# A fused attention and SiLU feed-forward kernel: the first two units of tokens take the ff chunks in two halves, and 14 instead of 10 heads stay in plain float32

## The chip, the cores and the metric

The kernel runs on one core of one Trainium2 chip. The metric is the device time of one execution in microseconds (us), lower is better. The kernel before took 1336.0 us as the median of three runs (1329.97 to 1337.23).

## The reference, cut to what matters

```python
# q, k, v: (8, 8, 576, 64); M_prev: (8, 8, 64, 64); z_prev: (8, 8, 64); beta: (8,)
scores = scale * np.matmul(q, k.transpose(0, 1, 3, 2))      # causal mask
a = np.exp(scores - max); a /= a.sum(-1, keepdims=True) + 1e-09
local = np.matmul(a, v)
q_p = phi(q)                                                # elu + 1
mem_out = einsum(q_p, M_prev) / (einsum(q_p, z_prev) + 1e-06)
attn = g * mem_out + (1 - g) * local                        # g = sigmoid(beta), per head
x = attn.transpose(0, 2, 1, 3).reshape(4608, 512)
h = x @ w_in                                                # 512 x 2048
out = (h * sigmoid(h)) @ w_out                              # 2048 x 512, float32
```

The weights `w_in` and `w_out` arrive as 64-bit floats; everything else is float32.

## The kernel before, in words

There are 64 heads (8 batches of 8), and one head is one round of `attention()`. In the same round the first part of head n (`scores`: transposes of q and k, score matmuls, mask and row minimum, exponentials, row sums, scaling) is interleaved with the second part of head n-1 (`values`: transposes of the probabilities, product with v and with M_prev, result into `xt`). One round is 10 steps of the generator.

A head is made in one of two ways. A **whole** head (the first `N_WHOLE`) keeps float32 operands: two matmul instructions stand for each float32 product, and there is little elementwise work. Its score matmuls have k and q transposed in 64 rows (`qf`, `tt[0:64]`). A **split** head writes each operand as a high and a low fp32r part, stacked to 128 rows (`kk`, `qq`, `ql`, `ph`, `pl`, `vs`, `qp`): fewer TensorE cycles, but more work on ScalarE (ACT), VectorE (DVE) and GpSimd (POOL).

The feed-forward part (`ffn()`) works on units of 256 tokens, 18 units in all. A unit goes over 8 pairs of ff chunks. One pair is 24 matmuls into `h` (L552, 128x256), then tanh on ACT (L563), one operation on DVE (L564), one on POOL (L567), one on DVE (L568), and 12 matmuls into `acc` (L532, 128x512). I call these 36 matmuls one **FFN step**; a unit is 8 steps. A unit needs all heads of the batches that its tokens lie in: units 0 and 1 need the first 8 heads, units 2 and 3 the first 16, units 4 and 5 the first 24, and so on (`heads_needed`).

Before any chunk of weights is used it is **prepared** (`split_weight`): its 64-bit words are turned into float32 and split into a high and a low part. There are 32 such chunks, 16 of `w_in` and 16 of `w_out`, each with three operations on DVE (L152, L154, L159), three on ACT (L150, L158, L161) and two on POOL (L156, L162). 12 of the 32 do not stay on the chip: they go to DRAM and come back for every use through two buffers named `flow`.

The order of the work is set in two places. The loop at the end of the function paces the three generators against each other: `PREP_RATE` chunks are prepared per 9 attention steps, `FFN_RATE` and `FIRST_RATE` say how many FFN steps go with an attention step. A scheduler then lays the recorded instructions out into one fixed order for each engine. All DMAs are issued from one queue (SP).

Of the kernel before, what the change touches and what calls it, by code (L numbers as in the profile page):

```python
# [8 lines left out]
F32 = mybir.dt.float32  # L9
# [3 lines left out]
AF = mybir.ActivationFunctionType  # L13
ALU = mybir.AluOpType
# [11 lines left out]
NB = dict(vs=1, e=2, r=1, qp=1, ms=2, raw=1, qn=2, mr=3, zb=2, st=2, nrm=2, ph=2, pl=2, xb=1, tt=2)  # L26
PS_S, PS_T, PS_X, PS_H = 2, 2, 1, 1
FIRST_STEPS = 1
N_WHOLE = 10
ROW_BUFS = 4  # L30
W_AHEAD = 2
PREP_RATE = 3.0
PREP_AFTER = 3.0
FFN_RATE = 0.22
FIRST_RATE = 0.2
FIRST_UNITS = 2
W_EARLY = 2

# [2 lines left out]
def memory_attention_then_silu_ffn(ctx, tc, q, k, v, M_prev, z_prev, beta, w_in, w_out, out):  # L41
    nc = tc.nc
    B, H, S, D = q.shape
    NT, DM = out.shape
    DFF = w_in.shape[1]
    P = 128
# [94 lines left out]
    def split_weight(kind, c, raw):  # L141
# [24 lines left out]
    ready, anchor = set(), {}  # L166


    order = [
        (kind, 2 * x + j) for p in range(NP + 1) for kind, x in (("i", p), ("o", p - 1))  # L170
        if 0 <= x < NP for j in range(2)]
    loaded = []

    def load_next(n):
# [40 lines left out]
    def scores(b, h, raw, rest, made, whole):  # L215
# [5 lines left out]
        anchor["dve"] = nc.vector.transpose(out=tt, in_=raw.rearrange("p c e -> p (c e)")).ins  # L221
        if whole:
            qq = pool.tile([P, S], F32, tag="kk", name="qf", bufs=QK_BUFS)
            nc.scalar.copy(qq[0:64], tt[64:P])
            terms = [(qq[0:64], tt[0:64])]
        else:
            kk = pool.tile([P, S], F32R, tag="kk", name="kk", bufs=QK_BUFS)
            qq = qrow[h % QK_BUFS]
            ql = qlow[h % QK_BUFS]
            nc.scalar.copy(kk[0:64], tt[0:64])  # L230
            nc.scalar.copy(qq[64:P, 0:S], tt[64:P])  # L231
            nc.gpsimd.tensor_tensor(out=kk[64:P], in0=tt[0:64], in1=f(kk[0:64]), op=ALU.subtract)
            nc.scalar.copy(qq[0:64, 0:S], tt[64:P])
            for low, x0, x1 in ((ql[0:64], 0, S - LAST), (qq[0:64, S:S + LAST], S - LAST, S)):
                nc.gpsimd.tensor_tensor(  # L235
                    out=low, in0=tt[64:P, x0:x1], in1=f(qq[64:P, x0:x1]), op=ALU.subtract)
            nc.scalar.copy(qq[:, S + LAST:], f(qq[:, S - LAST:S]))
            terms = [(qq, kk), (ql, kk)]
# [25 lines left out]
        for side, other, x0, x1, o in ((slice(0, LAST), slice(LAST, P), 0, SPLIT, P),  # L264
                                       (slice(LAST, P), slice(0, LAST), SPLIT, S, 0)):
            s = ps_s.tile([P, 512], F32, tag="s", name="s")
            s = s[:, 0:x1 - x0]
            row = pair[side, o:o + x1 - x0]
            more = mask[side, 0:x1 - x0] if x1 < S else mask[side, 4 * P + x0 - x1:]
            if whole:  # L270
                nc.tensor.matmul(s[side], qq[0:64, S - LAST:S], tt[0:64, x0:x1], start=True, stop=True)
            else:
                q0 = S - LAST if side.start == 0 else S
                nc.tensor.matmul(s, qq[:, q0:q0 + P], kk[:, x0:x1], start=True, stop=True)
                nc.scalar.copy(row, s[other])
                if x1 == S:
                    nc.gpsimd.tensor_tensor(
                        out=row[:, x1 - x0 - LAST:], in0=row[:, x1 - x0 - LAST:], in1=mask[side, 4 * P - LAST:],
                        op=ALU.add)
                more = row  # L280
            halves.append((s[side], row, more, st[side, 5:6]))
# [190 lines left out]
                second = values(b, h, made, xt[b, h // 2], n < N_WHOLE)  # L472


    flow_order = [(kind, 2 * p + j) for p in range(NP + 1) for kind, p in (("i", p), ("o", p - 1)) for j in range(2)]
    flow_order = [x for _ in range(NU) for x in flow_order if x in FLOW]
    flowing = []

    def flow():
# [30 lines left out]
    def heads_needed(u):  # L510
        return ((u + 1) * T - 1) // S * H + H

    def ffn():
        ahead = None
        for _ in range(FLOW_BUFS):
            yield from flow()
        for u in range(NU):
            while done[0] < heads_needed(u):
                yield "wait"
            xu = ahead or split_x(u)  # L520
            ahead = None
            bank, tag = (ps_s, "s") if done[0] == B * H and u % 2 else (ps_a, "a")
            acc = [bank.tile([P, DM], F32, tag=tag, name="acc") for _ in range(T // P)]

            def second(p, g):
                for c in range(2):
                    w = fetch("o", 2 * p + c)
                    for t in range(T // P):
                        at = slice(t * P, (t + 1) * P)
                        terms = [(g[:, gi, c, at], w[:, wi]) for gi, wi in ((0, 0), (0, 1), (1, 0))]  # L530
                        for n, (ta, tb) in enumerate(terms):
                            nc.tensor.matmul(  # L532
                                acc[t], ta, tb, start=p == 0 and c == 0 and n == 0,
                                stop=p == NP - 1 and c == 1 and n == len(terms) - 1)
                    if ("o", 2 * p + c) in FLOW:
                        yield from flow()

            before = None
            for p in range(NP):
                while not {("i", 2 * p), ("i", 2 * p + 1)} <= ready:  # L540
                    yield "prepare"
                if done[0] == B * H and p % 2:
                    h = ps_t.tile([P, 2, T], F32, tag="t", name="h")
                else:
                    h = ps_h.tile([P, 2, T], F32, tag="h", name="h")
                for c in range(2):
                    w = fetch("i", 2 * p + c)
                    w4 = w.rearrange("p a (k f) -> p a k f", f=P)
                    for kk in range(KD):
                        terms = [(w4[:, wi, kk], xu[kk][:, xi]) for wi, xi in ((0, 0), (0, 1), (1, 0))]  # L550
                        for n, (ta, tb) in enumerate(terms):
                            nc.tensor.matmul(  # L552
                                h[:, c], ta, tb, start=kk == 0 and n == 0,
                                stop=kk == KD - 1 and n == len(terms) - 1)
                    if ("i", 2 * p + c) in FLOW:
                        yield from flow()
                yield
                if before:
                    yield from second(*before)

                h = h.rearrange("p c t -> p (c t)")
                th = pool.tile([P, 2 * T], F32, tag="row", name="th", bufs=ROW_BUFS)
                nc.scalar.activation(th, h, AF.Tanh, scale=0.5)  # L563
                nc.vector.scalar_tensor_tensor(out=th, in0=th, scalar=1.0, in1=h, op0=ALU.add, op1=ALU.mult)  # L564
                g = pool.tile([P, 2, 2, T], F32R, tag="g", name="g", bufs=G_BUFS)
                hi, lo = (g[:, j].rearrange("p c t -> p (c t)") for j in range(2))
                nc.gpsimd.tensor_scalar(hi, th, 1.0, 1.0, op0=ALU.mult, op1=ALU.mult)  # L567
                nc.vector.tensor_tensor(out=lo, in0=th, in1=f(hi), op=ALU.subtract)  # L568
                while not {("o", 2 * p), ("o", 2 * p + 1)} <= ready:
                    yield "prepare"  # L570
                before = p, g
                if p == NP - 2 and u + 1 < NU and done[0] >= heads_needed(u + 1):
                    ahead = split_x(u + 1)
                yield
            yield from second(*before)
            for t in range(T // P):
                o = pool.tile([P, DM], F32, tag="row", name="o", bufs=ROW_BUFS)
                nc.scalar.activation(o, acc[t], AF.Copy, scale=0.5)
                r0 = u * T + t * P
                nc.sync.dma_start(out=out[r0:r0 + P, :], in_=o)  # L580
            yield

    A_STEPS, F_STEPS = 9, 2 * NP + 1
    att, prep, prod = attention(), preparation(), ffn()
    steps, produced, steps_made = 0, 0.0, 0
    going = True
    while going:
        going = next(att, "end") != "end"  # L590
        steps += 1
        started = done[0] >= H
        while going and len(ready) < min(2 * KF, steps * (PREP_AFTER if started else PREP_RATE) / A_STEPS):
            next(prep)
        if started:
            produced += (FFN_RATE if steps_made >= FIRST_UNITS * F_STEPS else FIRST_RATE) * F_STEPS / A_STEPS
        while going and produced >= 1.0:
            said = next(prod, "end")
            if said == "wait":
                produced = min(produced, 1.0)  # L600
                break
            if said == "prepare":
                next(prep)
                continue
            produced -= 1.0
            steps_made += 1
# [28 lines left out]
```

## Time and profile before

| what | value |
|---|---|
| median of three runs | 1336.0 us |
| profiled execution | 1331.87 us |
| its span on the core | 1330.1 us |
| granted TensorE clock, mean | 0.978 |
| median time to landing, 256 KB store of `o` | 4.2 us |
| median time to landing, 512 KB load of a chunk of `w_in` | 4.4 us |

The profiled execution has its own time; the span is what the engines cover, and 1.8 us lie around it. Times inside the span are read from its start. PE is TensorE's matmuls, PEld its weight loads. In a row of the timeline stand start, duration, engine, line, operation, output<-inputs, shapes and count, and in brackets the idle time before it with what ended it. In a row of the groups, "| 45.5, 1469 |" means 45.5 us busy in all and 1469 ns for one. The windows give, for a stretch A:B, the busy time of each engine with its count, then the granted clock, the DMA share and GB/s.

### The profile page before, as it was taken

The page shows a single profiled execution, that of the slowest core. Times are in us where ns is not written, and L with a number is a line of the kernel's source. Part 1 is how long each engine was busy: PE and PEld are TensorE (multiplying, and loading weights), DVE is VectorE, ACT ScalarE, POOL GpSimd, SP SyncE. Part 2 cuts the span into 40 slices and gives each one's busy share as a digit, 9 for nine tenths or more (in the row PEclk, how much of TensorE's full clock was granted, in tenths as well). Part 3 has the DMA queues.
Part 4 walks back from the last instruction along what each step waited for, and adds up shares of the span by engine and source line. Part 5 has one row for each costly group of instructions (what it writes and reads, how often), then busy time and mean ns, then how long its engine had stood idle before and what let it go on. Part 6 is the DMA issues. An engine that isn't in the chain of part 4 may idle for free.

```text
span 1330.1 us, 24649 instructions
## 1 busy us (share of the span) xinstructions
PE 1269.9 (95%) x7858; PEld 1084.7 (82%) x7858; DVE 963.4 (72%) x2580; ACT 805.2 (61%) x1999; POOL 798.1 (60%) x1169
## 2 busy tenths in 40 slices
PE   6988989999999999999999999999999999999998
PEld 2343458898989899899989898989898889899997
DVE  7988985788888878877888787778878875322222
ACT  6777765667676767667776676666767663111111
POOL 6888994676666667766677665656576653101110
PEclk9986799999999999999999999999999999999999
DMA  6766555554555545555555455455545432444444
GB/s 163 191 177 176 151 152 159 136 140 134 135 150 137 151 116 135 152 137 151 136 149 140 136 139 136 131 149 136 137 134 145 128 101 80 155 137 155 156 159 143
DMA packets 302994, 190.39 MB, mean 143 GB/s; under 512 B 258832, under 2 KB 267024, under 8 KB 302864
## 3 DMA queue, kind: packets, MB, share of 16 engines
q1 hardware_dynamic: 302864, 188.82, 50.8%
q8 instruction: 62, 1.02, 0.3%
q14 instruction: 68, 0.56, 0.1%
HBM read 173.02 MB, written 15.73 MB: 142 GB/s over the span
## 4 chain that ended last, share of the span: by engine, by line
PE 71%; DVE 13%; ACT 6%; DMA 4%; issue 3%; POOL 2%; SPq 1%; DVEq 0%; POOLq 0%; ACTq 0%
PE h L552 27%; PE acc L532 24%; PE x L422 7%; PE s L250 5%; PE tp L376 4%; DVE s L252 2%; PE x L414 1%; PE tq L351 1%; DMA zb<-in_z_prev 1%; DVE xu L505 1%; DMA flow<-wo_s 1%; DVE th L564 1%; DVE wy L152 1%; DVE wy L159 1%; ACT p L254 1%
## 5 line engine op out<-in xcount | busy, mean ns | idle before, releaser
L552 PE MATMUL h<-xu,wi 128*128 128x256 f32 x2592 | 373.8, 287 | 10.0 <-DVE th L564 7.3
L552 PEld LDWEIGHTS h<-xu,wi 128*128 128x128 f32 x2592 | 342.6, 191 | 24.9 <-DVE th L564 5.9
L304 POOL TENSOR_SCALAR p<-p,st 128x384 f32<-128x384 f32 (+3 forms) x320 | 186.1, 600 | 127.4 <-DVE st L302 121.2
L532 PE MATMUL acc<-wo,g 128*128 128x512 f32 x864 | 244.8, 399 | 0.0
L567 POOL TENSOR_SCALAR g<-th 128x512 fp32r<-128x512 f32 x144 | 90.9, 631 | 236.8 <-DVE th L564 205.7
L532 PE MATMUL acc<-flow,g 128*128 128x512 f32 x864 | 230.9, 395 | 0.7 <-DMA flow<-wo_s 0.7
L254 ACT ACTIVATE p<-s,st 128x128 f32<-128x128 f32 (+3 forms) x256 | 134.9, 528 | 123.2 <-DVE st L252 93.7
L564 DVE SCALAR_TENSOR_TENSOR th<-th,h 128x512 f32<-128x512 f32 x144 | 98.5, 685 | 130.5 <-ACT th L563 128.0
L532 PEld LDWEIGHTS acc<-flow,g 128*128 128x128 f32 x864 | 158.9, 188 | 33.9 <-DMA flow<-wo_s 1.8
L532 PEld LDWEIGHTS acc<-wo,g 128*128 128x128 f32 x864 | 150.0, 189 | 20.1 <-POOL p L304 0.5
L563 ACT ACTIVATE th<-h 128x512 f32<-128x512 f32 x144 | 85.6, 595 | 128.1 <-PE h L552 127.3
L407 DVE TENSOR_TENSOR pl<-tp,ph 128x384 fp32r<-128x384 f32 x216 | 118.4, 550 | 38.1 <-ACT ph L406 33.9
L568 DVE TENSOR_TENSOR g<-th,g 128x512 fp32r<-128x512 f32 x144 | 104.8, 728 | 50.5 <-POOL g L567 49.3
L252 DVE CUSTOM_DVE_ANT_0 s<-s,mask 128x128 f32<-128x128 f32 (+3 forms) x256 | 125.4, 492 | 11.5 <-PE s L250 6.7
L376 PE MATMUL tp<-ident,p 128*128 128x128 f32 x640 | 123.0, 292 | 8.5 <-DVE qp L359 3.7
L552 PE MATMUL h<-xu,flow 128*128 128x256 f32 x864 | 126.7, 284 | 0.0
L406 ACT CAST ph<-tp 128x384 fp32r<-128x384 f32 x216 | 104.7, 490 | 23.6 <-PE x L422 14.7
L552 PEld LDWEIGHTS h<-xu,flow 128*128 128x128 f32 x864 | 114.1, 190 | 0.9 <-issue 0.3
L376 PEld LDWEIGHTS tp<-ident,p 128*128 128x128 f32 x640 | 81.5, 147 | 37.4 <-POOL p L304 9.3
L235 POOL TENSOR_TENSOR ql<-tt,qq 64x512 fp32r<-64x512 f32 x54 | 73.2, 1356 | 20.6 <-ACT qq L231 11.3
L328 POOL TENSOR_TENSOR r<-e,zb 128x320 f32<-128x320 f32 x64 | 59.8, 935 | 42.4 <-DVE e L327 35.4
L422 PE MATMUL x<-pl,vs 128*128 128x256 f32 x324 | 81.7, 307 | 0.0
(103 smaller groups left out, 2430.2 us busy)
## 6 DMA issues: line engine op xcount, KB each, us to landing
flow<-wo_s SPq DMA_DIRECT2D x144, 512.0 KB, 3.5
flow<-wi_s SPq DMA_DIRECT2D x72, 512.0 KB, 3.8
raw<-in_k SPq DMA_DIRECT2D x128, 72.0 KB, 2.3
raw<-in_q SPq DMA_DIRECT2D x128, 72.0 KB, 2.5
out<-o SPq DMA_DIRECT2D x36, 256.0 KB, 4.2
wraw<-in_moe_w_in SPq DMA_DIRECT2D x16, 512.0 KB, 4.4
qn<-in_q SPq DMA_DIRECT2D x64, 128.0 KB, 2.9
vr<-in_v SPq DMA_DIRECT2D x64, 128.0 KB, 2.6
```

Of the source, the lines that this page charges most:

```text
L252: anchor["dve"] = nc.vector.tensor_tensor_reduce(s, s, mask[:, 3 * P - P * i:], QS, 3.0e38, ALU.add, ALU.min, st[:, i:i + 1]).ins
L254: nc.scalar.activation(pt, s, AF.Exp, bias=st[:, i:i + 1], scale=-1.0, accum_out=st[:, 10 + i:11 + i])
L304: nc.gpsimd.tensor_scalar(pb[x], pb[x], st[:, 15 + x:16 + x], 1.0, op0=ALU.mult, op1=ALU.mult)
L376: nc.tensor.transpose(t[:, o:o + P], pb[i][:, P * j:P * j + P], ident)
L406: nc.scalar.copy(ph[:, 0:o], t[:, 0:o])
L407: nc.vector.tensor_tensor(out=pl[:, 0:cut], in0=t[:, 0:cut], in1=f(ph[:, 0:cut]), op=ALU.subtract)
L422: nc.tensor.matmul(x[0:rows, q0:n], vs[0:n_k, j], part[0:n_k, o:o + n - q0], start=False, stop=last)
L532: nc.tensor.matmul(acc[t], ta, tb, start=p == 0 and c == 0 and n == 0, stop=p == NP - 1 and c == 1 and n == len(terms) - 1)
L552: nc.tensor.matmul(h[:, c], ta, tb, start=kk == 0 and n == 0, stop=kk == KD - 1 and n == len(terms) - 1)
L564: nc.vector.scalar_tensor_tensor(out=th, in0=th, scalar=1.0, in1=h, op0=ALU.add, op1=ALU.mult)
L567: nc.gpsimd.tensor_scalar(hi, th, 1.0, 1.0, op0=ALU.mult, op1=ALU.mult)
L568: nc.vector.tensor_tensor(out=lo, in0=th, in1=f(hi), op=ALU.subtract)
```

## The change

Four things are changed together.

- The first two units no longer run one after the other through all 8 pairs. A list `runs` says (unit, first pair, end pair): unit 0 takes pairs 0 to 3, unit 1 takes pairs 0 to 3, then unit 1 takes pairs 4 to 7, then unit 0 takes them. After the first half the sums (`acc`, times 0.5) go to DRAM tiles `sums`; after the second half they are loaded again and added on DVE. So the first half of the work on two units needs 16 chunks of weights, and `order`, in which chunks are loaded and prepared, follows that use.
- Weights are prepared more slowly at first (`PREP_RATE` 2.0) and faster once 8 heads are done (`PREP_AFTER` 8.0). `FIRST_RATE` goes from 0.2 to 0.6.
- 14 heads instead of 10 are whole.
- In a whole head, the score matmuls take all 128 rows: `qf` has zeros in rows 64 to 127 (a memset on POOL), and `tt` is taken with all its rows, whose lower half (q transposed) meets those zeros.

```diff
-N_WHOLE = 10
+N_WHOLE = 14
-PREP_RATE = 3.0
-PREP_AFTER = 3.0
+PREP_RATE = 2.0
+PREP_AFTER = 8.0
-FIRST_RATE = 0.2
+FIRST_RATE = 0.6
...
+    runs = [(0, 0, NP // 2), (1, 0, NP // 2), (1, NP // 2, NP), (0, NP // 2, NP)]
+    runs += [(u, 0, NP) for u in range(2, NU)]
+    uses = [
+        (kind, 2 * x + j) for u, p0, p1 in runs for p in range(p0, p1 + 1)
+        for kind, x in (("i", p), ("o", p - 1)) if p0 <= x < p1 for j in range(2)]
+    order = sorted(set(uses), key=uses.index)
+    sums = [dram.tile([T // P, P, DM], F32, name=f"sum{u}") for u in range(2)]
...
+            nc.gpsimd.memset(qq[64:P], 0.0)
             nc.scalar.copy(qq[0:64], tt[64:P])
-            terms = [(qq[0:64], tt[0:64])]
+            terms = [(qq, tt)]
...
-                nc.tensor.matmul(s[side], qq[0:64, S - LAST:S], tt[0:64, x0:x1], start=True, stop=True)
+                nc.tensor.matmul(s[side], qq[:, S - LAST:S], tt[:, x0:x1], start=True, stop=True)
...
-        for u in range(NU):
+        for n_run, (u, p0, p1) in enumerate(runs):
...
-            for p in range(NP):
+            for p in range(p0, p1):
...
-                nc.scalar.activation(o, acc[t], AF.Copy, scale=0.5)
-                nc.sync.dma_start(out=out[r0:r0 + P, :], in_=o)
+                dest = out[r0:r0 + P, :] if p1 == NP else sums[u][t]
+                if p0:
+                    nc.sync.dma_start(out=o, in_=sums[u][t])
+                    nc.vector.scalar_tensor_tensor(
+                        out=o, in0=acc[t], scalar=0.5, in1=o, op0=ALU.mult, op1=ALU.add)
+                else:
+                    nc.scalar.activation(o, acc[t], AF.Copy, scale=0.5)
+                nc.sync.dma_start(out=dest, in_=o)
...
-        while going and len(ready) < min(2 * KF, steps * (PREP_AFTER if started else PREP_RATE) / A_STEPS):
+        while going and prepared < min(2 * KF, int(asked)):
             next(prep)
+            prepared += 1
+        asked = max(asked, prepared) + (PREP_AFTER if started else PREP_RATE) / A_STEPS
```

How the fixed orders differ is seen at three places. The first is POOL at the start of the program, while heads 0 and 1 are made: `wy` and `wi`, `wo`, `flow` are pieces of prepared chunks (two rows for each chunk), `p` are probabilities, `r` and `e` belong to the memory part. Before, from the scaling of head 0's probabilities to the start of that of head 1:

```order
L304 TENSOR_SCALAR p_254<-p_254,st 128x384
L156 TENSOR_TENSOR wy<-wy,wraw 128x512
L334 TENSOR_TENSOR e<-e,nrm 128x320
L156 TENSOR_TENSOR wy<-wy,wraw 128x512 x2
L162 TENSOR_TENSOR wi_116<-wy,wi_116 128x512
L156 TENSOR_TENSOR wy<-wy,wraw 128x512
L328 TENSOR_TENSOR r<-e,zb 128x320
L162 TENSOR_TENSOR flow<-wy,flow 128x512
L162 TENSOR_TENSOR wo_130<-wy,wo_130 128x512
L334 TENSOR_TENSOR e<-e,nrm 128x320
L156 TENSOR_TENSOR wy<-wy,wraw 128x512
L162 TENSOR_TENSOR flow<-wy,flow 128x512
```

The same stretch of the changed program:

```order
L311 TENSOR_SCALAR p_235<-p_235,st 128x384
L162 TENSOR_TENSOR wi_115<-wy,wi_115 128x512
L230 MEMSET qf 64x576
L156 TENSOR_TENSOR wy<-wy,wraw 128x512
L335 TENSOR_TENSOR r<-e,zb 128x320
L156 TENSOR_TENSOR wy<-wy,wraw 128x512
L162 TENSOR_TENSOR wi_116<-wy,wi_116 128x512
L156 TENSOR_TENSOR wy<-wy,wraw 128x512
L341 TENSOR_TENSOR e<-e,nrm 128x320
```

Between the two heads stand nine operations on weights before and five now, and one memset of `qf` has come in.

The second place is TensorE (PE) where head 10 begins, its first score matmul being the first row of each piece. Before, head 10 is split (`kk`, `qq`, `ql`):

```order
L250 MATMUL s<-kk,qq_150 128x128
L250 MATMUL s<-kk,ql_154 128x128
L376 MATMUL tp<-ident,p_1478 128x128
L376 MATMUL tp<-ident,p_1491 128x128 x2
L393 MATMUL tp<-ident,p_1517 128x2x64
L250 MATMUL s<-kk,qq_150 128x256
L250 MATMUL s<-kk,ql_154 128x256
```

The changed program, where head 10 is whole (`qf`, `tt`, `vr`, `mr`):

```order
L257 MATMUL s<-tt,qf 128x128
L429 MATMUL x<-ph,vr 64x320
L383 MATMUL tp<-ident,p_1334 128x128
L383 MATMUL tp<-ident,p_1346 128x128 x2
L383 MATMUL tp<-ident,p_1371 128x128
L383 MATMUL tp<-ident,p_1384 128x128 x2
L400 MATMUL tp<-ident,p_1399 128x2x64
L257 MATMUL s<-tt,qf 128x256
```

One float32 product stands in place of two fp32r ones, and nothing of the FFN has moved ahead of it: in both programs 24 matmuls into `h` stand before the first score matmul of head 10. Ahead of the first mask operation of head 10 on DVE there stand the three operations of 31 chunks before, and of 20 now.

The third place is PE where the changed program has head 16 in work and the FFN work on units 0 and 1 comes to its end; `h` and `acc` are FFN rows, all others are attention:

```order
L560 MATMUL h<-xu,wi_114 128x256 x9
L540 MATMUL acc<-wo_144,g 128x512 x6
L540 MATMUL acc<-flow,g 128x512 x6
L257 MATMUL s<-kk,qq_150 128x384
L257 MATMUL s<-kk,ql_154 128x384
L257 MATMUL s<-kk,qq_150 128x512
L257 MATMUL s<-kk,ql_154 128x512
L421 MATMUL x<-qp,ms 128x256
L383 MATMUL tp<-ident,p_3189 128x128
L383 MATMUL tp<-ident,p_3204 128x128 x2
L383 MATMUL tp<-ident,p_3223 128x128
L281 MATMUL s<-kk,qq_150 128x256
```

Before, at the same head, FFN and attention still alternate:

```order
L250 MATMUL s<-kk,qq_150 128x128
L250 MATMUL s<-kk,ql_154 128x128
L552 MATMUL h<-xu,flow 128x256 x12
L532 MATMUL acc<-wo_138,g 128x512
L376 MATMUL tp<-ident,p_2879 128x128
L376 MATMUL tp<-ident,p_2895 128x128
L384 MATMUL tp<-swapped,p_2915 128x128
L532 MATMUL acc<-wo_138,g 128x512 x3
L250 MATMUL s<-kk,qq_150 128x256
L250 MATMUL s<-kk,ql_154 128x256
L532 MATMUL acc<-wo_138,g 128x512 x2
```

In the changed program a piece of 36 attention matmuls without any of the FFN begins behind the `acc` rows, and at heads 24 to 26 there is one of 42. Before, the longest such piece from head 14 on has 20. (A split head has 41 attention matmuls.)

More of the change, by code (lines that the diff above doesn't have):

```diff
@@ L166, in memory_attention_then_silu_ffn @@
     ready, anchor = set(), {}
-    order = [
-        (kind, 2 * x + j) for p in range(NP + 1) for kind, x in (("i", p), ("o", p - 1))
-        if 0 <= x < NP for j in range(2)]
+    runs = [(0, 0, NP // 2), (1, 0, NP // 2), (1, NP // 2, NP), (0, NP // 2, NP)]
[5 more added lines that the diff above has]
+    sums = [dram.tile([T // P, P, DM], F32, name=f"sum{u}") for u in range(2)]
     loaded = []
@@ L472, in attention @@
                 second = values(b, h, made, xt[b, h // 2], n < N_WHOLE)
-    flow_order = [(kind, 2 * p + j) for p in range(NP + 1) for kind, p in (("i", p), ("o", p - 1)) for j in range(2)]
-    flow_order = [x for _ in range(NU) for x in flow_order if x in FLOW]
+    flow_order = [x for x in uses if x in FLOW]
     flowing = []
@@ L516, in ffn @@
             yield from flow()
-        for u in range(NU):
+        for n_run, (u, p0, p1) in enumerate(runs):
             while done[0] < heads_needed(u):
                 yield "wait"
-            xu = ahead or split_x(u)
+            if n_run == 0 or runs[n_run - 1][0] != u:
+                xu = ahead or split_x(u)
             ahead = None
+            later = runs[n_run + 1][0] if n_run + 1 < len(runs) else u
             bank, tag = (ps_s, "s") if done[0] == B * H and u % 2 else (ps_a, "a")
@@ L532, in second @@
                             nc.tensor.matmul(
-                                acc[t], ta, tb, start=p == 0 and c == 0 and n == 0,
-                                stop=p == NP - 1 and c == 1 and n == len(terms) - 1)
+                                acc[t], ta, tb, start=p == p0 and c == 0 and n == 0,
+                                stop=p == p1 - 1 and c == 1 and n == len(terms) - 1)
                     if ("o", 2 * p + c) in FLOW:
@@ L571, in ffn @@
                 before = p, g
-                if p == NP - 2 and u + 1 < NU and done[0] >= heads_needed(u + 1):
-                    ahead = split_x(u + 1)
+                if p == p1 - 2 and later != u and done[0] >= heads_needed(later):
+                    ahead = split_x(later)
                 yield
@@ L586, in memory_attention_then_silu_ffn @@
     att, prep, prod = attention(), preparation(), ffn()
-    steps, produced, steps_made = 0, 0.0, 0
+    asked, prepared, produced, steps_made = 0.0, 0, 0.0, 0
     going = True
@@ L590, in memory_attention_then_silu_ffn @@
         going = next(att, "end") != "end"
-        steps += 1
         started = done[0] >= H
-        while going and len(ready) < min(2 * KF, steps * (PREP_AFTER if started else PREP_RATE) / A_STEPS):
+        while going and prepared < min(2 * KF, int(asked)):
             next(prep)
+            prepared += 1
+        asked = max(asked, prepared) + (PREP_AFTER if started else PREP_RATE) / A_STEPS
         if started:
@@ L603, in memory_attention_then_silu_ffn @@
                 next(prep)
+                prepared += 1
                 continue
```

## The prediction

> **What bounds the kernel now.** I read the page first: how busy the engines are, and where in the span they are not.
>
> ```profile
> PE 1269.9 (95%) x7858; PEld 1084.7 (82%) x7858; DVE 963.4 (72%) x2580; ACT 805.2 (61%) x1999; POOL 798.1 (60%) x1169
> PE   6988989999999999999999999999999999999998
> PEclk9986799999999999999999999999999999999999
> ```
>
> A slice is 33 us. From the seventh on, TensorE is full at full clock: there only its own work counts. The first six (200 us) are different: holes in PE, and a granted clock that falls to 0.6. The windows say who is busy there (PE, PEld, DVE, ACT, POOL, then clock and DMA).
>
> ```profile
> 10.00:67.00 57.00, 51.38 (x108) 20.30 (x109) 48.47 (x116) 40.81 (x98) 45.57 (x44) 1.00 0.71 189
> 67.00:175.00 108.00, 91.00 (x289) 42.95 (x288) 95.49 (x213) 82.76 (x198) 94.07 (x85) 0.76 0.59 161
> 10.00:175.00 165.00, 142.38 (x395) 63.24 (x396) 143.96 (x329) 123.57 (x296) 139.64 (x128) 0.84 0.63 171
> 175.00:205.00 30.00, 29.17 (x171) 21.37 (x171) 23.17 (x52) 20.76 (x54) 28.27 (x33) 1.00 0.67 179
> 326.00:1090.00 764.00, 743.97 (x5004) 680.72 (x5002) 620.08 (x1758) 526.82 (x1334) 510.44 (x805) 1.00 0.51 138
> ```
>
> From 10 to 175 us, DVE (0.87), PE (0.86) and POOL (0.85) are bound together. But PE's busy time there is inflated. The timeline of PE shows the same pair of score matmuls at two speeds, and one whole head at the fast one (from the `tq` transposes at 66.66 to those at 79.23):
>
> ```profile
> 43.37 2.07 PE L250 MATMUL s<-tt,qf 64*128 64x512 f32 x2
> 75.69 1.12 PE L250 MATMUL s<-tt,qf 64*128 64x512 f32 x2
> 66.66 0.90 PE L351 MATMUL tq<-ident,e 128*128 128x128 f32 x3
> 79.23 0.55 PE L351 MATMUL tq<-ident,e 128*128 128x128 f32 x3
> ```
>
> So at 43 us the clock is really halved, although its row says 1.00 before the first change. A whole head costs PE 12.6 us there with a few FFN matmuls and the slow first rows; I take 11.4 warm and about twice that cold.
>
> For the sum I cut the span on PE at the first score matmul of heads 10, 18 and 63:
>
> ```profile
> 179.08 0.31 PE L250 MATMUL s<-kk,qq 128*128 128x128 f32 x1
> 326.38 0.22 PE L250 MATMUL s<-kk,qq 128*128 128x128 f32 x1
> 1089.97 0.33 PE L250 MATMUL s<-kk,qq 128*128 128x128 f32 x1 [1.00 <-DVE st L284]
> ```
>
> A = 179.1, B = 147.3, C = 763.6, D = 240.1 us, together the span of 1330.1. The price of FFN work is read from starts in the tail, where PE has nothing else:
>
> ```profile
> 1308.78 1.60 PE L552 MATMUL h<-xu,flow 128*128 128x256 f32 x12
> 1310.22 1.53 PE L532 MATMUL acc<-wo,g 128*128 128x512 f32 x6
> 1311.59 2.08 PE L552 MATMUL h<-xu,wi 128*128 128x256 f32 x16
> ```
>
> 12 `h` take 1.44 us (0.120 each), 6 `acc` 1.37 (0.229 each); an FFN step is 5.6 us. C holds 2112 `h` and 1056 `acc`, 495 us, so its 45 split heads cost 268 / 45 = 6.0 us each, stalls included.
>
> **The change part by part.**
>
> *Fewer chunks ahead of head 10 (A).* By the order, 20 chunks instead of 31 are prepared before head 10's first mask operation. A chunk costs:
>
> ```profile
> L156 POOL TENSOR_TENSOR wy<-wy,wraw 128x512 uint32<-128x512 uint32 x31 | 45.5, 1469 | 10.2 <-ACT xt L425 3.6 <-DMA wraw<-in_moe_w_out 2.4 <-DVE wy L154 2.1
> L154 DVE SCALAR_TENSOR_TENSOR wy<-wraw,wy 128x512 uint32<-128x512 uint32 x30 | 29.1, 974 | 0.5
> L159 DVE SCALAR_TENSOR_TENSOR wy<-wraw,wy 128x512 f32<-128x512 f32 x31 | 28.5, 927 | 2.3 <-POOL wy L156 2.2
> L152 DVE TENSOR_SCALAR wy<-wraw 128x512 uint32<-128x512 uint32 x30 | 21.4, 716 | 1.1 <-DMA wraw<-in_moe_w_in 0.8
> L162 POOL TENSOR_TENSOR flow<-wy,flow 128x512 fp32r<-128x512 f32 x9 | 12.9, 1433 | 0.0
> L84 POOL MEMSET mask<- 128x512 f32 x1 | 0.5, 530 | 0.0
> ```
>
> On DVE 0.716 + 0.974 + 0.927 = 2.62 us, on POOL 1.47 + 1.43 = 2.9. Eleven chunks take 28.8 us off DVE and 32 off POOL. POOL gets about ten memsets of 64x576, at the row of the 128x512 one 5 us, so 27 net. Each memset waits until the score matmuls of two heads earlier have freed its buffer, and the scaling of probabilities stands behind it in POOL's queue; the order puts it well ahead of its head, so I add nothing; a wait of 1 us at each would be 10.
> Between 10 and 179.1 us DVE is busy 143.96 and 4.1/30 of 23.17, that is 147.1 us; 118.3 remain. At the share of 0.87 they take 136 us (A = 146), at 0.95 124.5 (A = 134.5). I take 0.90, since PE, which now makes DVE wait, gets lighter (next point): 131.5 us, **A = 142**.
>
> *Scores 128 rows high.* The time of a float32 matmul does not go by its rows:
>
> ```profile
> L422 PE MATMUL x<-ph,vr 128*64 128x320 f32 x60 | 28.2, 559 | 1.7 <-ACT ph L401 1.7
> L414 PE MATMUL x<-qp,mr 64*64 64x320 f32 x20 | 9.2, 544 | 3.8 <-ACT xt L425 3.8
> ```
>
> 559 and 544 ns: the doubled height costs nothing by itself. What it may change is the clock. Ten heads in A's 132 us leave 13.2 us each, enough for warm heads (11.4) and not for cold ones. Before, PE was nine tenths busy from 10 to 67 us (51.38 of 57) and still cold. A dense stretch that stayed cold, and the one ahead of the turn at 67 us:
>
> ```profile
> 35.00 1.97 PE L422 MATMUL x<-ph,vr 128*64 128x320 f32 x4
> 36.90 1.22 PE L250 MATMUL s<-tt,qf 64*128 64x256 f32 x2
> 38.05 1.73 PE L422 MATMUL x<-ph,vr 128*64 128x320 f32 x4
> ...
> 40.54 1.65 PE L250 MATMUL s<-tt,qf 64*128 64x384 f32 x2
> ...
> 63.29 3.44 PE L422 MATMUL x<-ph,vr 128*64 128x320 f32 x8
> ```
>
> The first has 64-row scores in between, the second is 3.4 us of 128-row products alone. So I expect 128-row scores to keep PE warm most of the time. The Trainium skill has a rule against this: by "TensorE: Matmul & The Clock Gate", Part 1, the clock is released by how busy TensorE was in a window of about 3.4 us, and nothing is said of rows. By it the height would change nothing; the busy but cold 57 us above speak against it. What that case gives is the first rival.
>
> *Whole heads 10 to 13, and the halves (B).* The order has 408 `h` and 192 `acc` between the two cuts instead of 384 and 192: 49 + 44 = 93 us. Four whole heads at 11.4 are 45.6 (four split ones were 24), four split ones 23.8: 162.4 us of PE. Before, the same sum is 90.1 + 47.7 = 137.8 against 147.3 measured; 9.5 us were lost while POOL was full (28.27 of 30). Now the twelve late chunks lie here: over heads 10 to 12 DVE has 12 x 2.62 + 3 x 7.0 (its remaining 65 us of 10 to 175 over 9.3 heads) + 6 FFN steps at 1.41 = 61 us beside 69 of PE. They fit, tightly: 4 us lost, between 0 and the 9.5 of before.
>
> *The FFN catches up with the heads.* Units 2 and 3 must wait for 16 heads, units 4 and 5 for 24. The order shows two pieces of about one head each where PE has attention alone. DVE needs for a split head without FFN:
>
> ```profile
> L568 DVE TENSOR_TENSOR g<-th,g 128x512 fp32r<-128x512 f32 x144 | 104.8, 728 | 50.5 <-POOL g L567 49.3
> L564 DVE SCALAR_TENSOR_TENSOR th<-th,h 128x512 f32<-128x512 f32 x144 | 98.5, 685 | 130.5 <-ACT th L563 128.0
> ```
>
> 620.08 / 45 = 13.8 us per head, less 1.96 FFN steps x 1.41, is 11.0, against 6.0 of PE: 5 us lost for each piece. It is nothing if DVE has worked ahead, and twice that if the clock falls too. So **B = 162.4 + 4 + 5 = 171**.
>
> *C and D.* C gets 24 `h` and 24 `acc` more (8.4 us) and the second piece (5): **777**. D loses 48 and 24 (11.3): **229**.
>
> *Sums in DRAM.* Four stores and four loads of 256 KB, and four DVE operations like L564 in place of four ACT copies (2.7 us, hidden beside PE). The nearest row is the store of `o`:
>
> ```profile
> out<-o SPq DMA_DIRECT2D x36, 256.0 KB, 4.2
> ```
>
> A load that comes late holds up DVE's queue, the masks of the next head and the FFN's operations in it: nothing if it is early, 4.2 us for each of two units if not. By SP's order each pair of loads stands right behind the last weight load of its half, ahead of the sums' end; I take 0.
>
> **Sum:** 142 + 171 + 777 + 229 = 1319 us of span; with the 1.8 us around it 1321, against 1331.9 for the profiled execution (which is 4 us under the median of the three runs).
>
> **The rivals.**
>
> *The clock stays as it was.* For it: the change adds no PE work to A, and the chip's rule need not see rows. Then PE's busy time in 10 to 179 stays at 146 us; at a share of 0.95 that is 154, A = 164, and the time 1343: slower, since 11 us of profit turn into 11 of loss. It decides at A = 153, when PE needs over 13.6 us a head, that is when more than a fifth of the work of heads 0 to 9 is done cold. Against it: the 128-row stretch before the turn at 67 us.
>
> *The two lone pieces and the crowded heads cost double.* B and C grow by 4 + 5 + 5: 1335, no change. For it: the clock falls to 0.76 where PE starves. Against it: `tt` and the probabilities have two buffers, so DVE and ACT can run a head ahead.
>
> *Nothing starves.* DVE reaches 0.95 in A (134.5), and the lone pieces cost nothing: 1319 - 7.5 - 10 + 1.8, 1303.
>
> *The halves do not do what they say.* The FFN does not start earlier by the order: 24 `h` before head 10 in both. Only the deferred chunks make A shorter. This is in the sum already.
>
> **Chances.** My forecast 0.50 (its own range 1312 to 1330), clock as it was 0.25, double cost 0.12, nothing starves 0.13. About 0.5% (6.7 us) is what a measurement of this kernel can tell from no change. Seven tenths of my own case, and the last, are faster by more than that: 0.48. The clock's case gives 0.20 slower, its milder part no change. The range goes from the last rival's time to the first's, 1303 to 1343.
>
> **What would show it.** On the chip, head 10's first score matmul at 142 us (146 if DVE keeps 0.87, 164 if PE is cold); the 512-wide score pair at 1.1 us rather than 2.1 for most of heads 0 to 9; head 18 about 171 us after head 10; holes of PE only in heads 16 and 24 to 26. The forecast is wrong if A is over 153 us, or if the lone pieces cost over 10 us each.

## The result, and the profile after

The changed kernel takes 1343.0 us, the median of 6 runs (1340.72 to 1345.27), beside 1334.8 for the kernel before in the same session: a ratio of 1.006, 95% interval 1.0036 to 1.0083. The change costs about 8 us; 1321 was forecast. The profiled execution took 1340.72 us, its span 1338.9, 8.8 more than before.

The page of the changed kernel (busy time of each engine, then two rows of the 40 slices, in tenths):

```profile
PE 1268.9 (95%) x7878; PEld 1079.6 (81%) x7878; DVE 958.9 (72%) x2552; ACT 795.0 (59%) x1987; POOL 786.5 (59%) x1147
PE   5879989998999899999999999999999999999998
PEclk9997999998999899999999999999999999999999
```

In the first six slices PE is no busier than before, but its clock is higher. The 10th and the 14th slice (302 to 335 and 435 to 469 us), full before, now have holes in both rows. The cuts of the prediction, in PE's timeline:

```profile
143.22 0.46 PE L257 MATMUL s<-tt,qf 128*128 128x128 f32 x2
326.27 0.22 PE L257 MATMUL s<-kk,qq 128*128 128x128 f32 x1
1112.18 0.22 PE L257 MATMUL s<-kk,qq 128*128 128x128 f32 x1
```

| us | before | forecast | after | after less before | after less forecast |
|---|---|---|---|---|---|
| A, to head 10 | 179.1 | 142 | 143.2 | -35.9 | +1.2 |
| B, heads 10 to 17 | 147.3 | 171 | 183.0 | +35.8 | +12.0 |
| C, heads 18 to 62 | 763.6 | 777 | 785.9 | +22.3 | +8.9 |
| D, tail | 240.1 | 229 | 226.7 | -13.4 | -2.3 |
| span | 1330.1 | 1319 | 1338.9 | +8.8 | +19.9 |

A came as forecast, but head 18 starts at 326.27 against 326.38 before: B gave all of it back, for 24 more `h` (2.9 us). The windows of the changed kernel for A, heads 10 to 13, 14 to 17, 24 to 27 and the rest of C (busy PE, PEld, DVE, ACT, POOL, then granted clock, DMA share, GB/s):

```profile
10.00:143.22 133.22, 109.33 (x414) 52.69 (x414) 118.87 (x303) 105.69 (x268) 109.79 (x114) 0.94 0.64 169
143.22:246.76 103.54, 96.09 (x506) 65.47 (x507) 78.74 (x168) 65.02 (x153) 74.44 (x79) 0.98 0.61 177
246.76:326.27 79.51, 75.70 (x462) 64.36 (x459) 53.13 (x150) 45.98 (x121) 36.66 (x58) 0.96 0.56 155
437.04:515.84 78.80, 74.33 (x476) 66.72 (x474) 61.66 (x175) 50.66 (x129) 49.78 (x78) 0.96 0.48 127
515.84:1112.18 596.34, 579.74 (x3864) 527.76 (x3862) 481.68 (x1358) 406.58 (x1032) 402.89 (x624) 0.99 0.50 135
```

The same stretches of the kernel before, A, heads 10 to 13 and 14 to 17, then 24 to 27 and the rest of C:

```profile
10.00:179.08 169.08, 146.46 (x418) 65.82 (x419) 146.88 (x334) 127.56 (x306) 143.72 (x132) 0.85 0.63 171
179.08:260.91 81.83, 78.54 (x498) 65.43 (x496) 57.45 (x155) 51.42 (x131) 54.58 (x79) 1.00 0.57 154
260.91:326.38 65.47, 64.51 (x434) 58.66 (x432) 53.95 (x158) 46.36 (x119) 45.65 (x70) 1.00 0.50 130
424.65:491.90 67.25, 64.90 (x431) 59.58 (x429) 53.77 (x155) 47.00 (x118) 43.47 (x69) 0.97 0.48 130
491.90:1089.97 598.07, 582.10 (x3922) 532.58 (x3920) 483.87 (x1374) 410.98 (x1043) 399.75 (x630) 1.00 0.51 138
```

In A, PE's busy time falls by 37 us for the same matmuls, and DVE by 28.0: eleven chunks' work went elsewhere. In B, PE was nearly full at full clock before; now it idles 7.5 and 3.8 us, and the clock is below 1.

**How stalls are counted below.** Where the expectations speak of an excess, it is the time between two head starts, less the price of the FFN matmuls that the order puts there, less 11.4 or 6.0 us for each head that begins there. That has a fault, which the runs brought out: when a head begins, the second parts of about two heads before it are still to come, and where those are whole and the next heads split, the window holds more work than its heads. So the table also has **stalls**: the same, with attention counted by the columns of the matmuls that the order really puts there (scaled to 6.0 and 11.4 a head; an estimate, good to some 2 us). F is the time of head 18's start less the price of all FFN matmuls ahead of it. Executions of the kernel before differ by a few us in span, and so smaller differences mean nothing.

| kernel | span | A | B | C | D | F | stalls 10-17 | 18-27 | 28-62 |
|---|---|---|---|---|---|---|---|---|---|
| before | 1330.1 | 179.1 | 147.3 | 763.6 | 240.1 | 233.4 | 1.4 | 0.1 | -0.3 |
| after | 1338.9 | 143.2 | 183.0 | 785.9 | 226.7 | 230.4 | 12.5 | 6.0 | 6.3 |
| e1 | 1344.6 | 144.2 | 180.7 | 789.9 | 229.8 | 232.0 | 35.6 | 4.7 | 10.3 |
| e2 | 1347.0 | 158.5 | 181.2 | 780.6 | 226.7 | 243.9 | 11.0 | 0.2 | 6.2 |
| e3 | 1333.1 | 169.2 | 156.6 | 766.9 | 240.4 | 232.9 | 9.7 | -0.6 | 3.5 |
| e4 | 1343.4 | 149.8 | 185.6 | 781.4 | 226.7 | 231.1 | 6.8 | 5.4 | 10.5 |
| e5 | 1335.0 | 143.0 | 184.5 | 781.0 | 226.5 | 231.7 | 14.4 | 0.7 | 6.1 |
| e6 | 1354.5 | 177.6 | 164.8 | 771.6 | 240.5 | 249.5 | -2.3 | 4.0 | 3.9 |
| e7 | 1339.2 | 150.7 | 189.5 | 769.3 | 229.7 | 236.0 | 18.3 | -0.5 | 10.4 |
| e8 | 1331.3 | 143.7 | 184.3 | 767.8 | 235.5 | 232.1 | 13.7 | 0.3 | 1.9 |
| e9 | 1343.3 | 169.3 | 162.2 | 771.5 | 240.2 | 238.6 | 6.5 | 6.9 | -0.3 |
| e10 | 1316.8 | 153.9 | 151.4 | 771.2 | 240.3 | 212.4 | 5.2 | 7.7 | -1.3 |
| e11 | 1325.5 | 158.9 | 152.7 | 774.0 | 239.8 | 218.7 | 5.0 | 8.7 | 0.4 |
| e12 | 1331.6 | 144.5 | 182.8 | 765.4 | 238.9 | 223.1 | 6.5 | -1.0 | 15.3 |
| e13 | 1342.5 | 181.0 | 146.9 | 852.7 | 161.8 | 235.0 | 1.0 | -1.0 | 7.6 |

### The profile page after: what moved, and what is told of

Same layout as the page of the kernel before. It is cut to its first block, busy times and chain, and to the rows that moved or that the text cites. A ratio compares the mean times of both kernels' runs of the same rounds, so it can differ in the third digit from the quotient of the medians.

```text
span 1338.9 us, 24619 instructions
## 1 busy us (share of the span) xinstructions
PE 1268.9 (95%) x7878; PEld 1079.6 (81%) x7878; DVE 958.9 (72%) x2552; ACT 795.0 (59%) x1987; POOL 786.5 (59%) x1147
## 4 chain that ended last, share of the span: by engine, by line
PE 53%; DVE 8%; ACT 5%; issue 3%; POOL 2%; DMA 2%; SPq 0%; DVEq 0%; POOLq 0%; ACTq 0%
PE h L560 21%; PE acc L540 20%; PE x L429 4%; PE s L257 3%; PE tp L383 3%; DMA flow<-wo_s 1%; DVE s L259 1%; DVE th L572 1%; DVE pl L414 1%; POOL p L311 1%; DVE xu L511 1%; ACT p L261 1%; PE tq L358 1%; PE x L421 1%; DVE tt L227 1%
## 5 line engine op out<-in xcount | busy, mean ns | idle before, releaser
L540 PE MATMUL acc<-wo,g 128*128 128x512 f32 x864 | 240.6, 398 | 0.5 <-DVE g L576 0.5
L572 DVE SCALAR_TENSOR_TENSOR th<-th,h 128x512 f32<-128x512 f32 x144 | 98.5, 684 | 133.5 <-ACT th L571 132.2
L571 ACT ACTIVATE th<-h 128x512 f32<-128x512 f32 x144 | 85.8, 596 | 144.2 <-PE h L560 142.7
L576 DVE TENSOR_TENSOR g<-th,g 128x512 fp32r<-128x512 f32 x144 | 121.4, 843 | 52.9 <-POOL g L575 51.7
L414 DVE TENSOR_TENSOR pl<-tp,ph 128x384 fp32r<-128x384 f32 x200 | 109.3, 552 | 24.5 <-ACT ph L413 21.4
L413 ACT CAST ph<-tp 128x384 fp32r<-128x384 f32 x200 | 96.5, 490 | 28.9 <-PE x L429 13.8
L242 POOL TENSOR_TENSOR ql<-tt,qq 64x512 fp32r<-64x512 f32 x50 | 68.7, 1374 | 34.5 <-issue 22.6
L239 POOL TENSOR_TENSOR kk<-tt,kk 64x576 fp32r<-64x576 f32 x50 | 74.6, 1492 | 9.4 <-ACT kk L237 6.6
```

Of the source, the lines that this page charges most:

```text
L413: nc.scalar.copy(ph[:, 0:o], t[:, 0:o])
L414: nc.vector.tensor_tensor(out=pl[:, 0:cut], in0=t[:, 0:cut], in1=f(ph[:, 0:cut]), op=ALU.subtract)
L540: nc.tensor.matmul(acc[t], ta, tb, start=p == p0 and c == 0 and n == 0, stop=p == p1 - 1 and c == 1 and n == len(terms) - 1)
```

## The experiments

**e1: the change with 10 whole heads.**

```diff
-N_WHOLE = 14
+N_WHOLE = 10
```

> The changed kernel with 10 whole heads instead of 14; all else of the change stays. Theory 1 (the whole heads' price on TensorE ate the gain): heads 10 to 13 cost 6.0 us each instead of 11.4, so from head 10's first score matmul to head 18's it is about 22 us shorter than the 183 us of the changed kernel, 161 us, and the time about 1321 us. Theory 2 (the elementwise engines are the bound there, since 12 late chunks and split heads meet: VectorE 31 + 33 + 8 us over three heads, 73 us against 52 us of TensorE): the same stretch stays at 178 to 188 us, with TensorE idle 15 us or more in it, and the time 1338 to 1348 us.

Measured: 1345.5 us, ratio 1.0095 (1.0067 to 1.0123); the ratios here and below are against the kernel before. A is that of the change, and B hardly shorter (180.7), although its four heads cost PE 22 us less. The window of heads 10 to 13 in e1:

```profile
144.23:238.06 93.83, 77.63 (x420) 60.75 (x419) 83.73 (x165) 66.14 (x156) 79.12 (x86) 0.89 0.58 166
```

PE idles 16.2 us at a clock of 0.89, while DVE is busy for 0.89 of the time and POOL for 0.84. As split heads these four need so much elementwise work, beside the deferred chunks, that PE waits; as whole heads they need PE. The excess here is 31.8, against 12.9 in the change. Either way head 18 comes at the same F.

**e2: the change with scores 64 rows high.**

```diff
-            nc.gpsimd.memset(qq[64:P], 0.0)
-            terms = [(qq, tt)]
+            terms = [(qq[0:64], tt[0:64])]
```

(and the same in the other score matmul)

> The changed kernel with the score matmuls of whole heads on 64 rows again, and without the memset; all else stays. If the 128 rows keep TensorE's clock up: the granted clock between 10 and 143 us falls from 0.94 to 0.85 or less, head 10's first score matmul comes at 154 to 164 us instead of 143.2, and the time rises by 8 to 20 us over the changed kernel. If the shorter first stage comes from the fewer chunks alone: head 10 begins at 140 to 145 us and the time is within 4 us of the changed kernel's.

Measured: 1353.1 us, ratio 1.0155 (1.010 to 1.0211); A 158.5. The window from 10 us to head 10 in e2:

```profile
10.00:158.53 148.53, 135.10 (x413) 59.80 (x413) 112.94 (x303) 105.58 (x266) 98.00 (x104) 0.80 0.58 151
```

The same matmuls take PE 135.1 us instead of 109.3, and A is 15.3 us longer. PE is busier here than in the change (0.91 of the time against 0.82), and yet has the lower clock. The Trainium skill, "TensorE: Matmul & The Clock Gate", Part 1, has the clock released by how busy PE was in a window of about 3.4 us; here the kernel with the busier PE is the slower clocked one, so busy time alone does not describe it.

**e3: before with scores 128 rows high, nothing else.**

```diff
+            nc.gpsimd.memset(qq[64:P], 0.0)
-            terms = [(qq[0:64], tt[0:64])]
+            terms = [(qq, tt)]
```

(and the same in the other score matmul)

> The kernel before with the 128-row scores (and the memset) alone. If the rows keep the clock up: TensorE's busy time between 10 and 179 us falls from 146 us to about 120, head 10's first score matmul moves from 179 to 165 to 174 us (VectorE, 147 us of work, is then the bound at a share of 0.9), and the time falls by 5 to 14 us. If the rows do nothing: the same as before within 4 us, or 5 us slower by the memsets on POOL.

Measured: 1335.4 us, ratio 1.0015 (0.9998 to 1.0032). The windows of A and of heads 10 to 13 in e3:

```profile
10.00:169.17 159.17, 120.09 (x414) 58.28 (x414) 147.33 (x326) 121.67 (x295) 137.23 (x132) 0.80 0.65 172
169.17:257.37 88.20, 80.32 (x479) 65.10 (x479) 66.70 (x169) 57.09 (x143) 67.41 (x88) 0.96 0.55 152
```

PE's busy time falls from 146.5 to 120.1 and A by 9.9 us, less than that, because DVE is now busy for 0.93 of it. The clock column of this row (0.80) cannot be compared with that of before (0.85): in before it reads 1.00 up to its first recorded change at 85 us, although the 512-wide score pairs of heads 0 to 3 take 1.9 to 2.1 us there. B gives 9.3 back: PE idles 7.9 us in heads 10 to 13 instead of 3.3.

**e6: before with 14 whole heads, nothing else.**

```diff
-N_WHOLE = 10
+N_WHOLE = 14
```

> The kernel before with 14 whole heads instead of 10 alone (64-row scores). Theory 1: from head 10's first score matmul to head 18's it takes 147.3 + 22 - up to 9.5 us that POOL's crowding cost before, 160 to 169 us, and the time is 12 to 22 us longer. Theory 2 (elementwise work is the bound there): the stretch gets no longer than 150 us, and the time is within 4 us of before or shorter.

Measured: 1359.0 us, ratio 1.0207 (1.0164 to 1.0249). The window of heads 10 to 13 in e6:

```profile
177.62:273.35 95.73, 95.73 (x499) 63.75 (x498) 44.66 (x130) 45.82 (x121) 35.93 (x53) 1.00 0.47 126
```

PE is busy without a gap at full clock, so nothing is lost here, and still the excess by heads is 5.1. That is work, by the fault in the counting that is described above: when head 10 begins, the products with v of two heads are still to come, when head 14 begins those of 1.2, and so the window holds 4.8 second parts. Without the other changes the four whole heads cost about their price of 21.6: the span grows by 24.4, B by 17.5 and C by 8.0.

**e4: FFN slower in the first two units; e7: the same with 12 whole heads.**

```diff
-FIRST_RATE = 0.6
+FIRST_RATE = 0.25
```

> The changed kernel with FIRST_RATE 0.25 instead of 0.6: the feed-forward work on the first units is spread over heads 9 to 16, so that by the fixed order no piece of attention longer than 21 matmuls without feed-forward work is left (36 at heads 16 to 17 and 42 at heads 24 to 26 in the changed kernel). If the two catch-ups cost what the sums left over (time between the cuts less the price of the matmuls: 7.6 us in heads 14 to 17 and 9.8 in heads 24 to 27 of the changed kernel, -0.7 and 1.3 in the kernel before): both fall under 3 us, and the time is 11 to 17 us under the changed kernel's, 1326 to 1332 us. If these holes only show time that TensorE must wait for the elementwise engines anyway: the waiting turns up between heads 10 and 14 or later, and the time stays within 5 us of the changed kernel's.

> The changed kernel with FIRST_RATE 0.25 and 12 whole heads. By the price of whole heads alone it is 2 x 5.4 = 11 us faster than the run with FIRST_RATE 0.25 and 14 whole heads. If the elementwise work between heads 10 and 14 is the bound with split heads (as in the run with 10 whole heads, where 18.9 of 21.6 us came back as idle TensorE), it is within 4 us of that run.

Measured: e4 1342.7 us, ratio 1.0057 (1.0034 to 1.008); e7 1338.7, 1.0034 (1.0015 to 1.0053). In e4 the order has no piece of attention alone at heads 16 and 17, and the excess of heads 14 to 17 goes from 7.6 to -0.7: that hole was the catch-up. It has none at heads 24 to 26 either (the longest from head 14 on is 18 matmuls), and there the excess goes from 9.8 to 4.1. But A is 6.5 us longer, and heads 28 to 62 have 10.5 us of stalls instead of 6.3; the total does not move. So the second expectation came out for the time: without these holes the kernel waits elsewhere. In e7 the stalls of heads 10 to 17 rise to 18.3: two split heads more, as in e1.

**e5: the change without halves.**

```diff
-    runs = [(0, 0, NP // 2), (1, 0, NP // 2), (1, NP // 2, NP), (0, NP // 2, NP)]
-    runs += [(u, 0, NP) for u in range(2, NU)]
+    runs = [(u, 0, NP) for u in range(NU)]
```

> The changed kernel with units 0 and 1 in one run each, so that the halves, the sums in DRAM and their order of weights are gone; the rates, the 14 whole heads and the 128 rows stay. If the halves do nothing of their own: head 10's first score matmul at 140 to 147 us, and the time within 5 us of the changed kernel's. If they let the feed-forward work start with 16 chunks and so spare waits: heads 10 to 13 take over 5 us longer for the same work and the time rises by 5 to 15 us.

Measured: 1339.0 us, ratio 1.0026 (1.0011 to 1.0041), A 143.0 as in the change, F 231.7. The halves bring nothing: A has the same length without them. Whether they cost up to 4 us, the intervals leave open.

**e8: the change with the FFN paced a little slower.**

```diff
-FFN_RATE = 0.22
+FFN_RATE = 0.215
```

> The changed kernel with FFN_RATE 0.215 instead of 0.22 alone: the order is the same up to head 20, and the piece of 42 attention matmuls without feed-forward work at heads 24 to 26 is gone. If that catch-up is what makes the changed kernel slower behind head 18: the time over the price of the matmuls in heads 24 to 27 falls from 9.8 us to under 3, and the time is 5 to 9 us under the changed kernel's, 1334 to 1338 us. If not: within 3 us of the changed kernel.

Measured: 1332.3 us, ratio 0.998 (0.9961 to 0.9998), 10.7 us under the change. Up to head 18 it is the change (F 232.1, stalls 13.7). Behind it the stalls fall from 12.3 us to 2.2. The windows of heads 24 to 27 and of the rest of C in e8:

```profile
439.54:504.53 64.99, 63.14 (x417) 57.35 (x416) 52.39 (x148) 44.67 (x114) 43.77 (x69) 0.97 0.52 132
504.53:1095.78 591.25, 576.03 (x3861) 527.14 (x3860) 484.21 (x1372) 407.48 (x1038) 398.67 (x624) 0.99 0.51 137
```

In heads 24 to 27 PE idles 1.9 us instead of 4.5, in the rest 15.2 instead of 16.6. The sum by columns gives 5.3 and 4.4 less of stalls; part of what idle time does not explain is the clock (0.96 in heads 24 to 27 of the change, 0.97 here), the rest is open. This kernel, like e12, lies barely under the one before.

This is how the hole looks in the changed kernel, in PE's timeline: the same score matmul early and in the hole, the waits around it, and the first FFN matmul afterwards:

```profile
442.83 0.34 PE L257 MATMUL s<-kk,qq 128*128 128x384 f32 x1
454.59 0.38 PE L257 MATMUL s<-kk,qq 128*128 128x256 f32 x1 [0.69 <-DVE st L291]
456.27 0.58 PE L421 MATMUL x<-qp,ms 128*128 128x256 f32 x1 [1.18 <-DVE xt L437]
456.75 0.69 PE L257 MATMUL s<-kk,qq 128*128 128x384 f32 x1
464.85 2.37 PE L560 MATMUL h<-xu,wi 128*128 128x256 f32 x15 [1.01 <-ACT xu L510]
```

And the window around it:

```profile
452.50:464.90 12.40, 9.17 (x41) 7.45 (x39) 9.74 (x34) 10.13 (x27) 6.59 (x12) 0.72 0.51 138
```

With no FFN beside it a head leaves PE short of work, PE waits for DVE, the clock drops, and the same matmul takes 0.69 us instead of 0.34. The FFN then waits another 1.0 for its own input.

**e13: the kernel before, with a catch-up put in.** Only the pace is raised, so that the FFN catches up with the heads at 31 to 33 (45 attention matmuls alone); the rows and whole heads are those of before.

```diff
-FFN_RATE = 0.22
+FFN_RATE = 0.26
```

> The kernel before with FFN_RATE 0.26 instead of 0.22 alone. The order is the same up to head 18; then the feed-forward work catches up with the heads once, at heads 31 to 33, where a piece of 45 attention matmuls appears that was not there. If a catch-up by itself costs time: the time over the price of the matmuls in heads 30 to 33 rises from about -1 us to 6 to 10 us, and the time by 5 to 10 us. If it was something else of the change (14 whole heads, the sums, the order of weights): no change within 3 us.

Measured: 1342.4 us, ratio 1.0064 (1.0041 to 1.0087). The first 28 heads are as before; heads 30 to 33 have an excess of 8.7 against -1.0. The windows across it:

```profile
580.00:590.00 10.00, 9.66 (x63) 8.45 (x61) 7.87 (x23) 7.00 (x16) 4.69 (x7) 1.00 0.42 125
590.00:600.00 10.00, 5.65 (x17) 3.61 (x17) 8.22 (x27) 7.62 (x20) 6.68 (x12) 0.62 0.61 157
600.00:610.00 10.00, 9.38 (x46) 8.34 (x46) 8.31 (x27) 7.57 (x22) 4.18 (x9) 0.70 0.18 32
```

PE idles 4.35 us in the second row, and the clock is low for these 20 us: a catch-up costs 8 to 10 us by itself, in a kernel that has nothing else of the change. (The faster pace also moves FFN work from D to C, and so these two columns of the table differ.)

**e9: e3 with 12 whole heads.**

```diff
-N_WHOLE = 10
+N_WHOLE = 12
```

> The kernel before with 128-row scores and 12 whole heads, no halves, rates as before. If up to head 18 the elementwise engines are the floor with 10 whole heads (three kernels with 10 whole heads came to 232 to 233 us for 18 heads and 32 chunks, feed-forward price taken off), two more whole heads take some 8 us off VectorE and add 11 us to TensorE, which has room: the same figure is 226 to 230 us and the time 4 to 8 us under that of before. If the price on TensorE counts in full: 243 us, and 10 us slower.

Measured: 1345.7 us, ratio 1.0078 (1.0052 to 1.0103). F grows by 5.7 over e3, half of the 10.8 that two whole heads cost PE; heads 18 to 27 lose another 7.5, and why is open.

**e10 and e11: e3 with less elementwise work for the weights.** e10 leaves out the operation that drops the smallest words (29 us of DVE in all), e11 the addition of the low part of each word (47 us of POOL); both kernels' weights are therefore others.

```diff
-            nc.vector.scalar_tensor_tensor(
-                out=w, in0=f(high), scalar=LEAST, in1=w, op0=ALU.is_ge, op1=ALU.mult)
```

```diff
-            nc.gpsimd.tensor_tensor(out=y, in0=y, in1=low, op=ALU.add)
```

> The kernel before with 128-row scores, and the last VectorE operation of each weight chunk (the product that drops the smallest weights, 32 x 0.92 = 29 us) left out. If VectorE is the floor of the first 18 heads: head 18's first score matmul less the price of the feed-forward work ahead of it falls from 233 us by 15 to 28 us, and the time by as much. If POOL or latency is: by under 8 us.

> The kernel before with 128-row scores, and POOL's first operation of each weight chunk (the addition of the low part, 32 x 1.47 = 47 us) left out. If VectorE is the floor of the first 18 heads: the same figure falls by under 8 us. If POOL is: by 15 us or more.

Measured, one time each: 1318.5 and 1327.3 us, beside 1334.5 for before in that session. F falls by 20.5 for the 29 us of DVE and by 14.2 for the 47 us of POOL. The second lies between its two expectations (under 8 with DVE as the floor, 15 or more with POOL). As far as one execution of each can tell, the start is bound by both: taking work from either shortens it, by 0.7 of what DVE and 0.3 of what POOL is spared. Less of it reaches the total, since heads 18 to 27 lose 7.7 and 8.7.

**e12: e8 with 13 whole heads.**

```diff
-FFN_RATE = 0.22
+FFN_RATE = 0.215
-N_WHOLE = 14
+N_WHOLE = 13
```

> The changed kernel with FFN_RATE 0.215 and 13 whole heads. By its fixed order neither catch-up is left: no piece of attention longer than 24 without feed-forward work behind head 10. If the catch-up at heads 16 and 17 costs what is over the price of the matmuls (7.6 us in heads 14 to 17) and a whole head 5.4 us on TensorE: 1332.3 - 7 - 3 = 1322 us, which is 1% under the kernel before. If the first 18 heads have a floor on VectorE and POOL that holds whatever the pacing: 1329 to 1335 us.

Measured: 1331.9 us, ratio 0.9981 (0.9965 to 0.9996). The total is where a fixed bound on the start puts it, but the trace does not bear that reason out: F is 223.1, 9 us under e8, and heads 10 to 17 have only 6.5 of stalls. The excess of 8.0 in heads 14 to 17 is nearly all the second part of head 12, the last whole one, and PE is almost full there:

```profile
231.98:327.31 95.33, 93.96 (x600) 82.25 (x599) 70.33 (x187) 57.21 (x144) 58.87 (x87) 0.98 0.60 168
491.31:1092.72 601.41, 579.26 (x3842) 526.14 (x3841) 479.40 (x1369) 406.89 (x1039) 404.48 (x625) 0.99 0.50 133
```

The gain is lost in heads 28 to 62 (second row), where PE idles 22.2 us against 15.2 in e8, in single stalls far apart (the largest at heads 54, 29 and 59). In 9.8 us of this idle time FFN matmuls into `h` wait for the DVE operation before them (L572), against 3.8 in e8; what holds DVE up there was not found.

## Why the prediction was wrong

**A was right, and for its reasons.** DVE was to have 118.3 us of work and be busy for 0.90 of the time; it had 118.87 in 133.22 (0.89). The share itself was a choice between 0.87 and 0.95, and e3 ran at 0.93. The 512-wide score pair takes 1.0 to 1.1 us in eight of heads 0 to 9, against six before. The memsets took 5.5 us for nine of 64x576, where 5 was assumed. That the height of the scores sets the clock is shown by e2 (A 15.3 longer without it) and e3 (PE's busy time 26 us less with nothing else changed). The first rival, the clock as it was, is out; that its time, 1343, is the measured one is chance, since it had A at 164.

**B's sum was built on a wrong reading.** "9.5 us were lost while POOL was full" is the step that failed. The row quoted for heads 10 to 13 of before shows only 3.3 us of idle PE at full clock; POOL is busy for 0.67 of it, and was full only in the 30 us that were quoted. The rest of the 9.5 was work: when head 10 begins, the second parts of the whole heads 8 and 9 are still to come, and a sum by heads that begin does not contain them. e6 shows the same, PE being full for all its 95.73 us and the sum by heads still 5.1 short. By columns the matmuls of B are 92.9 + 77.6 = 170.6 us, not 162.4. That is 8.2 of the 12.0 missing; with it alone the forecast would have been 1329. Most of the other 3.8 is a size: stalls of 12.5 where 4 + 5 stood. The first catch-up, at heads 16 and 17, was where it was forecast; e4, which has none there, takes it from an excess of 7.6 to -0.7.

**So the 36 us of A were not to be had in this way.** Before, B lost next to nothing (1.4), so nothing could be saved there. Deferring eleven chunks moves their elementwise work behind head 10. With split heads it starves PE (e1: 36 us of stalls). With whole heads PE has 22 us more to do, as e6 confirms, and 12.5 of stalls remain. Both put head 18 where it was: F is 230 to 236 in before, the change, e1, e3, e4, e5, e7 and e8. e10 and e11 show that it moves when elementwise work goes away rather than behind head 10. It is no hard bound: e12 is 7 us under this band, and what was lost there later has no name yet.

**"5 us lost for each piece" held for the head, not for the place.** With B giving back all of A, this is where time is lost. The second catch-up came in heads 24 to 26, as the order showed. The one head without FFN took 11.03 us (452.47 to 463.50), the 11.0 that was worked out. What was left out is what follows: the first FFN matmul waits for its input, and the clock has to come back. Heads 24 to 27 lost 6.9 by columns (1.3 before), and e13's catch-up 8.7. Beyond, heads 28 to 62 lost 6.3 (-0.3 before), where nothing was forecast, in single stalls far from the catch-up (the largest at heads 53, 62 and 58). e8 removes most of both with one number, the pace of the FFN, and nothing else: 10.7 us. That the catch-ups are all of the loss is not shown: e4 has neither of them and is no faster, and e1, e4 and e7, which have no such piece at heads 24 to 26, lose 10.3, 10.5 and 10.4 in heads 28 to 62. What makes these late stalls is open. The rest of C's miss is 1.6 us of attention work; D gave back 2.3.

**The rivals.** "Double cost" was the nearest, in its mechanism; its 14 us were less than the 19.9 because of the 8.2 above. The prediction gave 0.12 to it, and nothing to its standing together with a mispriced B. "Nothing starves" is out: PE idles 11.3 us in B. That the halves do nothing, as the order suggested, is borne out by e5.

**The sum after the fact**, against before: A -35.9; B whole heads 21.8, FFN 2.9, stalls 11.1; C FFN 8.4, attention 1.6, stalls 12.4 (5.8 and 6.6); D -13.4. Together that is +8.9, and the span grew by 8.8.

## What to carry to other kernels

Before a stall is put into a sum, look whether the engine is idle in that window: a shortfall of a price against a time can be work that the price did not count, most of all where a cut runs through overlapped rounds. Work deferred past a stage's end is gained only if the next stage has room on the engines that it needs; add up each engine over both stages. And where one stream can overtake another, pace it so that it never runs dry: the lost time is the hole, the wait for the first input and the slow clock after it, and a change of two per cent in one rate was worth 10.7 us here.

## What the runs showed of the hardware

Filling unused rows with zeros made TensorE faster in the first stage. Float32 score matmuls over 128 rows, half of them zeros, let the same matmuls of A run in 109.3 us of PE time instead of 135.1 (the change against e2), although PE was less busy; with nothing else changed (e3) it is 120.1 instead of 146.5. After a hole of some 4 us the clock stayed low for longer than the hole itself: 0.62 and 0.70 over the 20 us in e13, with PE busy for 0.94 of the second ten.
